# Two weight loads cut into three uneven pieces each, in a kernel of sparse attention and a spectral mix

## The chip, the cores and the metric

The kernel runs on one core of a Trainium2 chip. The metric is the device time of one execution in microseconds (us), as the median of several runs. The kernel before takes 432.17 us (three runs, 431.75 to 432.61). A further execution was profiled; its span, from the first to the last instruction, is 430.2 us. The engines are named as in the profile: PE is TensorE, DVE is VectorE, ACT is ScalarE, POOL is GpSimd and SP is SyncE.

## What is computed

Eight batches of eight heads go through a causal sparse attention. Four heads look at a local band and four at every 32nd position. The result is the input of a spectral mix. A Fourier transform runs along the sequence, 64 complex modes are each multiplied by a 512 by 512 complex matrix of their own, and the transform is inverted. A last product with `w_ch` follows.

```python
def _moe_ref(x, w_r, w_i, w_ch):                 # x: the attention's output, 8 x 576 x 512
    n_modes = w_r.shape[0]                       # 64
    X = np.fft.rfft(x, axis=1)
    Xr, Xi = (np.real(X[:, :n_modes]), np.imag(X[:, :n_modes]))
    Yr = np.einsum('bmd,mde->bme', Xr, w_r) - np.einsum('bmd,mde->bme', Xi, w_i)
    Yi = np.einsum('bmd,mde->bme', Xr, w_i) + np.einsum('bmd,mde->bme', Xi, w_r)
    Y[:, :n_modes] = Yr + 1j * Yi
    y = np.fft.irfft(Y, n=S, axis=1)
    u = x + y
    return u + np.maximum(u @ w_ch, 0.0)
    # ... cut: the attention, the shapes and the scaling of the inputs
```

The matrices `w_r` and `w_i` come as 32-bit numbers, 64 of 512 x 512 each. They are the bulk of what has to be read.

## The kernel before

The weights are loaded on GpSimd's queue, in pairs of modes and in halves of the input rows, and become 16-bit numbers on the way. A pair's tile has the real part on partitions 0 to 63 and the imaginary part on partitions 64 to 127. One load brings one part of one pair to 64 partitions: two modes of 4 rows of 512 numbers, that is 2 x 4 KB on a partition and 512 KB in all.

```python
    SPLIT1, SPLIT0 = 56, 48
    ORDER = [(1, m) for m in range(SPLIT1)] + [(0, m) for m in range(SPLIT0)]
    ORDER += [(1, m) for m in range(SPLIT1, NM)] + [(0, m) for m in range(SPLIT0, NM)]

    def w_fetch(n=1):
        for _ in range(n):
            i = len(w_tiles)                     # goes up by two with each pair
            if i >= 2 * NM:
                return
            half, m = ORDER[i]
            # ... cut: wt, the pair's tile, comes from a pool of five or from a borrowed place
            single = []
            for ri, src in enumerate((moe_w_r, moe_w_i)):
                dst = wt[ds(64 * ri, 64)]
                rows = src[m : m + 2, ds(256 * half, 256), :].rearrange(
                    "m (p c) e -> p m (c e)", c=4
                )
                dst = dst.rearrange("p m c e -> p m (c e)")
                ones = range(2)
                if ri and not m:
                    ones = [1]
                elif i < 2 * NM - 4:
                    nc.gpsimd.dma_start(dst, rows)          # L178
                    continue
                single += [(j, ri, dst[:, j], rows[:, j]) for j in ones]
            for _, _, to, rows in sorted(single, key=lambda x: x[:2]):
                nc.gpsimd.dma_start(to, rows)               # L182: one mode alone
            w_tiles.extend((wt[:, 0], wt[:, 1]))
```

A mode multiplies with sixteen small products and afterwards asks for the next pair:

```python
    def mode(slot, m):
        # ... cut
        for e in range(4):
            for c in range(4):
                nc.tensor.matmul(                           # L557
                    yv[:, mi, e, :],
                    wt[pr, XC[c], ds(128 * e, 128)],
                    Xh[half][pr, c, :, :, m],
                    start=(c == 0), stop=(c == 3),
                )
        if m % 2 and (slot or m // 2 not in GUEST):
            w_fetch()
        # ... cut
```

The inputs of the attention are loaded on the same queue. Those of the strided heads come as 64 partitions and, for every second batch, as 8 partitions more; those of the local heads come as 128 partitions.

```python
            if nb == 2:
                nc.gpsimd.dma_start(two[0:64], src[0:64])            # L210
            else:
                nc.gpsimd.dma_start(ring[0:64, n, :], src[0:64, b % 2])  # L212
            if b % 2 == 0:
                nc.gpsimd.dma_start(two[64:72], src[64:72])          # L214
    # ... cut: the local heads' load (L221), 128 partitions of 1152 numbers
```

Towards the end, modes and the work on the output rows alternate:

```python
    rest = [(0, m) for m in range(SPLIT1, NM)] + [(1, m) for m in range(SPLIT0, NM)]
    for i, (slot, m) in enumerate(rest):
        mode(slot, m)
        # ... cut: the next piece of the work on the output rows
    # ... cut: the last modes' spectra, the last product, the sums and the stores
```

Of the kernel before, what the change touches and what calls it, by code (L numbers as in the profile page):

```python
# [56 lines left out]
def kernel(  # L57
# [10 lines left out]
    nc = tc.nc  # L68
# [79 lines left out]
    SPLIT1, SPLIT0 = 56, 48  # L148
    ORDER = [(1, m) for m in range(SPLIT1)] + [(0, m) for m in range(SPLIT0)]
    ORDER += [(1, m) for m in range(SPLIT1, NM)] + [(0, m) for m in range(SPLIT0, NM)]  # L150
    w_tiles = []
    w_chs = {}
    w_ch = big.tile([128, 4, DM], F16, name="w_ch")

    def w_fetch(n=1):
        for _ in range(n):
            i = len(w_tiles)
# [3 lines that stand above are left out]
            if i // 2 in GUEST:  # L161
                wt = big.tile([128, 2, 4, DM], F16, tag=GUEST[i // 2], name="wt")
            else:
                wt = pw.tile([128, 2, 4, DM], F16, tag="w", name="wt")
# [9 lines that stand above are left out]
                ones = range(2)  # L174
                if ri and not m:
                    ones = [1]
                elif i < 2 * NM - 4:
                    nc.gpsimd.dma_start(dst, rows)  # L178
                    continue
                single += [(j, ri, dst[:, j], rows[:, j]) for j in ones]  # L180
            for _, _, to, rows in sorted(single, key=lambda x: x[:2]):
                nc.gpsimd.dma_start(to, rows)  # L182
            w_tiles.extend((wt[:, 0], wt[:, 1]))
# [362 lines left out]
    def mode(slot, m):  # L546
# [17 lines left out]
        if m % 2 and (slot or m // 2 not in GUEST):  # L564
            w_fetch()
# [144 lines left out]
    strided_tokens()  # L710
    load_str(2, 2)
    w_fetch()

    def str_front(b):
# [35 lines left out]
    for b in range(B):  # L750
        if b in (1, 3):
            load_str(b + 3, 2)
        load_loc(*[(), (), (), (), (0,), (1, 2), (3,), (4, 5)][b])
        w_fetch([2, 1, 1, 1, 1, 1, 0, 0][b])
        front = str_front(b + 1) if b + 1 < B else loc_front(0)
        for t in range(6):
            str_scores(b, t)
            if b > 0:
                if t < 2:
                    str_values(b - 1, 4 + t)  # L760
                elif t == 2:
                    dft(b - 1, 1)
            if t >= 2:
                str_values(b, t - 2)
            for w in front[SPLIT[t] : SPLIT[t + 1]]:
                w()
        if b == 1:
            nc.vector.memset(PL[:, 0:PS0], 0.0)
            fourier(0)
# [8 lines left out]
    for b in range(B):  # L778
# [12 lines left out]
        n = 0  # L791
        nm = NMODES[b]
        for mi in range(nm):
# [3 lines left out]
            n = upto  # L797
# [66 lines left out]
    n = 0  # L864
    for m in range(SPLIT0):
# [4 lines left out]
        n = upto  # L870
# [125 lines left out]
    n = 0  # L996
    NL = len(rest) - 2
    for i, (slot, m) in enumerate(rest):
# [4 lines left out]
        n = upto  # L1003
# [76 lines left out]
```

## Time and profile before

| | |
|---|---|
| time, median of 3 runs | 432.17 us |
| span of the profiled execution | 430.2 us |
| mean granted TensorE clock | 0.894 |
| busy: PE, DVE, ACT, POOL | 344.0, 236.3, 203.5, 107.4 us |
| moved by DMA | 91.78 MB, 213 GB/s in the mean |
| loads of pairs (L178): real, imaginary | 62 and 60 issues of 512 KB |
| issue to landing of those, median | 18.1 and 19.4 us |

The page cuts the span into 40 equal slices, of 10.75 us each. Its DMA row gives the mean busy share of the core's sixteen DMA engines in tenths, and the row below it what they moved. The chain that ended last is followed back from the last instruction, at each step to what released it. A line of the waits names the engine and line that waited, what it waited for, the total, the number of times and the longest one. In the chain told in order of time, a line has the start, the length and the work. The trace further keeps the time of every arrival that a load counts, and the start, length and bytes of every packet on a DMA queue, without the number of the DMA engine.

### The profile page before, as it was taken

Reading aid. Unit: us, or ns where it says so; the run is one execution under the profiler, and the core shown is the slowest. Engines: PE = TensorE matmul, PEld = TensorE weight load, DVE = VectorE, ACT = ScalarE, POOL = GpSimd, SP = SyncE. Lnnn points to the kernel's source line nnn. Section 1 sums busy time; section 2 is a strip of 40 time slices with the busy share of each in tenths; the row PEclk is TensorE's granted clock in tenths of the full one; section 3 lists DMA queues with packets and bytes.
Section 4 is the critical chain, followed back from the end, with each engine's and each line's share of the span. In section 5 each row is a group of like instructions: output and inputs, shape, how many; then the busy total and the mean of one; then the engine's idle time right before and its main releaser. Section 6 shows DMA issues by size and latency. Waiting matters only on the chain.

```text
span 430.2 us, 12274 instructions
## 1 busy us (share of the span) xinstructions
PE 344.0 (80%) x5420; PEld 238.3 (55%) x5420; DVE 236.3 (55%) x461; ACT 203.5 (47%) x357; POOL 107.4 (25%) x191
## 2 busy tenths in 40 slices
PE   2977878779988697898577767786897988888994
PEld 2865767658767575666345545454564544444331
DVE  3888778835544444534104334864684484444695
ACT  1777777634655354547131212522342463432773
POOL 8333332322432222221222221222222222210000
PEclk9999989955998889969755689999899998999998
DMA  8999999999999999999999999999999999992698
GB/s 150 213 213 213 214 214 210 212 210 212 214 213 214 214 213 214 213 214 211 214 214 214 214 213 214 213 214 213 213 213 213 214 214 214 213 206 53 223 353 304
DMA packets 30484, 91.78 MB, mean 213 GB/s; under 512 B 4000, under 2 KB 4768, under 8 KB 30432
## 3 DMA queue, kind: packets, MB, share of 16 engines
q0 software_dynamic: 24704, 81.28, 95.3%
q1 hardware_dynamic: 5216, 9.52, 6.2%
q8 instruction: 42, 0.69, 0.6%
q10 hardware_dynamic: 512, 0.21, 0.2%
q14 instruction: 10, 0.08, 0.0%
HBM read 162.83 MB, written 9.44 MB: 400 GB/s over the span
## 4 chain that ended last, share of the span: by engine, by line
DMA 69%; PE 20%; DVE 5%; issue 2%; ACT 2%; POOL 1%; DVEq 0%; ACTq 0%; POOLq 0%
DMA wt<-in_moe_w_i_dram 52%; DMA ring<-in_q_dram 7%; DMA ring<-in_v_dram 4%; DMA wt<-in_moe_w_r_dram 4%; PE y L557 3%; PE v L935 2%; PE u L945 2%; DMA ring<-in_k_dram 2%; PE v L958 1%; DVE yy L692 1%; PE sc L524 1%; PE sc L657 1%; DVE xb L233 1%; PE tp L405 1%; ACT v L243 1%
## 5 line engine op out<-in xcount | busy, mean ns | idle before, releaser
L557 PE MATMUL y<-X,wt 128*128 128x16 f16 (+1 forms) x2048 | 82.6, 193 | 37.1 <-DMA wt<-in_moe_w_i_dram 35.7
L557 PEld LDWEIGHTS <-wt 128*128 128x128 f16 (+1 forms) x2048 | 72.9, 102 | 51.4 <-issue 41.2
L178 POOL DMA_DIRECT2D wt<-in_moe_w_r_dram x62 | 36.4, 587 | 155.8 <-PE y L557 75.4
L178 POOL DMA_DIRECT2D wt<-in_moe_w_i_dram x60 | 35.4, 589 | 60.3 <-DMA wt<-in_moe_w_i_dram 49.7
L666 ACT ACTIVATE v<-sc 128x512 f16<-128x512 f32 x32 | 19.1, 597 | 64.9 <-PE sc L657 64.9
L481 ACT ACTIVATE PL<-sc 128x480 f16<-128x480 f32 (+1 forms) x48 | 27.2, 579 | 34.0 <-PE sc L467 33.7
L667 DVE COPY xo<-tp 128x512 f16<-128x512 f16 x32 | 22.1, 690 | 32.9 <-PE tp L665 32.8
L657 PE MATMUL sc<-w_cp,xT 128*128 128x512 f16 x128 | 38.3, 425 | 1.3 <-DVE xT L630 1.3
L233 DVE TENSOR_TENSOR xb<-av,rec 90x256 f16<-90x256 f32 (+2 forms) x80 | 36.0, 450 | 2.7
L232 DVE RECIPROCAL rec<-av 90x4 f32<-90x4 f32 (+2 forms) x80 | 14.6, 183 | 34.1 <-PE av L496 24.8
L412 DVE COPY qT<-tp 128x576 f16<-128x576 f16 x16 | 12.1, 758 | 33.4 <-PE tp L405 29.9
L904 DVE TENSOR_TENSOR xo<-u,xo 128x1024 f16<-128x1024 f32 x16 | 19.5, 1224 | 16.3 <-PE u L700 16.3
L243 ACT ACTIVATE v<-tp 128x640 f16<-128x640 f16 (+1 forms) x24 | 19.4, 808 | 19.0 <-PE tp L439 16.3
L405 PE MATMUL tp<-cI_s,ring 64*64 64x64 f16 x864 | 25.0, 204 | 2.0 <-issue 1.2
L370 ACT ACTIVATE PL<-sc 90x360 f16<-90x360 f32 (+1 forms) x48 | 22.8, 490 | 7.5 <-PE sc L363 7.1
L243 ACT ACTIVATE v<-v 128x1024 f16<-128x1024 f32 x16 | 16.4, 1025 | 19.4 <-PE v L700 19.3
L980 DVE TENSOR_TENSOR osb<-u,rl 128x1024 f32<-128x1024 f32 (+1 forms) x21 | 22.2, 1071 | 5.5 <-PE u L958 3.4
L451 PE MATMUL sc<-cMl_s,cI_s 128*128 128x480 f16 (+1 forms) x48 | 20.5, 426 | 3.6 <-ACT PL L481 2.0
L405 PEld LDWEIGHTS <-ring 64*64 64x64 f16 x864 | 19.5, 117 | 6.9 <-issue 2.9
L268 PE MATMUL tp<-cI_s,ring 72*128 72x72 f16 x256 | 15.3, 207 | 9.0 <-DMA ring<-in_v_dram 7.5
L972 ACT ACTIVATE rl<-v 128x1024 f32<-128x1024 f32 (+1 forms) x21 | 18.8, 902 | 6.6 <-PE u L958 4.1
L524 PEld LDWEIGHTS <-xb 108*128 108x128 f16 (+2 forms) x176 | 14.6, 103 | 11.6 <-DVE xb L233 7.1
(134 smaller groups left out, 696.2 us busy)
## 6 DMA issues: line engine op xcount, KB each, us to landing
wt<-in_moe_w_r_dram POOLq DMA_DIRECT2D x62, 512.0 KB, 18.1
wt<-in_moe_w_i_dram POOLq DMA_DIRECT2D x60, 512.0 KB, 19.4
out_dram<-osb SPq DMA_DIRECT2D x15, 512.0 KB, 3.2
ring<-in_v_dram POOLq DMA_DIRECT2D x8, 288.0 KB, 13.2
ring<-in_q_dram POOLq DMA_DIRECT2D x8, 288.0 KB, 13.6
ring<-in_k_dram POOLq DMA_DIRECT2D x8, 288.0 KB, 13.1
ring<-in_v_dram POOLq DMA_DIRECT2D x3, 512.0 KB, 14.8
ring<-in_q_dram POOLq DMA_DIRECT2D x3, 512.0 KB, 14.7
```

Source lines behind the costliest of these rows:

```text
L178: nc.gpsimd.dma_start(dst, rows)
L233: nc.vector.tensor_tensor(out=dst, in0=val.rearrange("p h (q c) -> p h c q", c=4), in1=rec[0:n, 0:pieces] .to_broadcast((n, pieces, 64)) . ...
L243: nc.scalar.activation(out=out, in_=in_, func=ACTF.Copy)
L370: nc.scalar.activation(out=PS[0:n, ds(POFF[t], 4 * n)], in_=scp[0:n, 0 : 4 * n], func=ACTF.Exp, scale=SCALE,)
L405: nc.tensor.transpose(tp[ds(64 * hp, 64), ds(64 * i, 64)], qn[ds(64 * hp, 64), ds(64 * (9 * g + i), 64)], idn[ds(64 * hp, 64), ds(64 * hp, ...
L451: nc.tensor.matmul(scp[:, 0 : n * times].rearrange("p (h x) -> p h x", h=times), idn, mask_rows("cMl", n, times), start=True, stop=False,)
L481: nc.scalar.activation(out=dst, in_=src, func=ACTF.Exp, scale=SCALE)
L557: nc.tensor.matmul(yv[:, mi, e, :], wt[pr, XC[c], ds(128 * e, 128)], Xh[half][pr, c, :, :, m], start=(c == 0), stop=(c == 3),)
L657: nc.tensor.matmul(vp, xT[:, ch], w_chs["cp"][:, ch, :], start=(ch == 0), stop=(ch == 3),)
L667: nc.vector.tensor_copy(out=xo.rearrange("p (h q c) -> p h q c", h=2, c=4), in_=tp[:, 0:512].rearrange("p (h c q) -> p h q c", h=2, c=4),)
L904: nc.vector.tensor_tensor(out=xo, in0=up[:, 0:n], in1=xo, op=AluOp.add)
L980: nc.vector.tensor_tensor(out=osb[:, j], in0=up[:, j], in1=rl[:, j], op=AluOp.add)
```

## The change

The real part of two pairs, the one that is fetched at index 56 and the one at index 86 of the order of modes, is no longer loaded by one transfer of 64 partitions. It is loaded by three, of 35, 20 and 9 partitions and of 7, 49 and 8. The same bytes go to the same places in the same order. The change is for the way in which a transfer is shared out among the DMA engines[...].

```diff
@@ -148,6 +148,7 @@
     ORDER += [(1, m) for m in range(SPLIT1, NM)] + [(0, m) for m in range(SPLIT0, NM)]
+    UNEVEN = {56: (35, 20, 9), 86: (7, 49, 8)}
     w_tiles = []
@@ -174,6 +175,12 @@
                 if ri and not m:
                     ones = [1]
+                elif i in UNEVEN and not ri:
+                    a = 0
+                    for n in UNEVEN[i]:
+                        nc.gpsimd.dma_start(dst[a : a + n], rows[a : a + n])
+                        a += n
+                    continue
                 elif i < 2 * NM - 4:
                     nc.gpsimd.dma_start(dst, rows)
                     continue
```

## The prediction

> **What bounds the kernel now.** I read the chain that ended last first, then the DMA rows, then who waits for whom in the last third, then the landings of single transfers.
>
> The page's chain, by engine and by line, and its DMA rows with the queues:
>
> ```profile
> DMA 69%; PE 20%; DVE 5%; issue 2%; ACT 2%; POOL 1%; DVEq 0%; ACTq 0%; POOLq 0%
> DMA wt<-in_moe_w_i_dram 52%; DMA ring<-in_q_dram 7%; DMA ring<-in_v_dram 4%; DMA wt<-in_moe_w_r_dram 4%; PE y L557 3%; PE v L935 2%; PE u L945 2%; DMA ring<-in_k_dram 2%; PE v L958 1%; DVE yy L692 1%; PE sc L524 1%; PE sc L657 1%; DVE xb L233 1%; PE tp L405 1%; ACT v L243 1%
> ...
> DMA  8999999999999999999999999999999999992698
> GB/s 150 213 213 213 214 214 210 212 210 212 214 213 214 214 213 214 213 214 211 214 214 214 214 213 214 213 214 213 213 213 213 214 214 214 213 206 53 223 353 304
> ...
> q0 software_dynamic: 24704, 81.28, 95.3%
> q8 instruction: 42, 0.69, 0.6%
> ```
>
> The stream of loads through GpSimd's queue (q0) is the bound: 213 GB/s without a hole until slice 36 (about 385 us), 69% of the chain. Nearly all of it is the weight pairs. The small line on q8 matters here: 42 packets of 16 KB (0.69 MB) that fetch instructions on the same sixteen DMA engines.
>
> The chain in order of time near the end of the loads:
>
> ```profile
> 344.12 19.38 DMA wt<-in_moe_w_i_dram
> 363.50 0.28 issue
> 363.79 19.38 DMA wt<-in_moe_w_i_dram
> 383.16 0.14 issue
> 383.30 0.64 PE y L557 x16
> ```
>
> The mode at 383.30 starts 0.14 us after a weight half has landed. From there TensorE works almost without a gap to the end at 430.2. So the landing at 383.16 sets the end, and 47.0 us (430.2 less 383.16) come after it whatever happens. Between 290 and 384 us TensorE does wait:
>
> ```profile
> PE y L557 <- DMA wt<-in_moe_w_i_dram: 11.3, 13, 2.1
> POOL wt L182 <- DMA wt<-in_moe_w_i_dram: 7.0, 4, 1.9
> ```
>
> That is 11.3 us in 13 waits, about 0.87 us each, one for nearly every pair of modes. TensorE follows the landings, so a shift of all landings there is a shift of the end.
>
> **How one transfer lands.** Each load counts sixteen arrivals, one from each DMA engine, and it is landed with the last. The trace keeps these arrivals. For an imaginary part early on they lie between 65.94 and 68.44 us, within 2.5 us. For the imaginary part that landed at 383.16 they begin at 376.26 and the offsets are 0, 0.46, 0.58, 0.71, 1.13, 1.46, 1.66, 2.72 and then 6.04, 6.07, 6.35, 6.41, 6.44, 6.47, 6.59, 6.91. Eight engines are ahead and eight lag by 5 to 7 us, though each got the same bytes. The packet records say why. A 4 KB packet starts every 0.305 us on an engine. At 53.89 us an instruction fetch takes 948 ns exactly where one engine's next packet was due, and that engine is 1.12 us late from then on. About five such fetches fall on each of eight engines: 5 x 1.12 = 5.6 us, the lag seen. So even shares end unevenly, and the last engine sets every landing. The mean of the sixteen offsets is 3.75 us, so perfect shares would gain 6.91 - 3.75 = 3.2 us.
>
> [...] The trace agrees for the 8-partition loads (L214): each puts two packets on eight engines and none on the other eight, and the next takes the other eight. [...] the next transfer's packet starts 21 ns after the packet that counts the arrival.
>
> **The change part by part.** The order of instructions on every engine stays; two loads on GpSimd become six.
>
> *More issues.* Each is 0.587 us by the row of L178, so four more cost GpSimd 2.3 us. GpSimd has only waits there. Eight semaphores go round the loads, so a load waits for the eighth before it; three pieces hold three of them, and for a while the queue holds six full loads instead of eight. Six times the 2.45 us from landing to landing is 14.7 us of stock, more than the 7 us between the first and the last engine. I book zero.
>
> *Moved shares.* [...] Normally an engine gets 4 partitions of such a load. [...] A partition is two packets, 0.61 us. So six engines get 3.05 us more, one 1.22 us, and eight get 2.44 us less.
>
> *If engines 8 to 15 are the laggards*, the largest lag falls to 6.91 - 2.44 = 4.47 us, and the six leaders go to at most 1.46 + 3.05 = 4.51 us. That is balanced to 0.04 us, so it is surely the intention: end 2.4 us earlier, 429.8 us.
>
> *But are they?* I followed the sixteen packet series through the 8-partition loads at 55 to 63 us, when five engines had had a fetch. Two of the five were in the group that L214 takes first (engines 0 to 7), three in the other. The later fetches that I could follow went to the other group, apart from one that I could not settle. So I count two laggards, perhaps three, among engines 0 to 7. Only engines 0 and 7 there are spared the 3.05 us. A laggard at 6.1 to 6.4 us that gets it stands at 9.2 to 9.5 us: 2.3 to 2.6 us over 6.91. Then the landing at 383.16 comes at 385.6 and the end 2.4 us later, 434.6 us.
>
> **The rivals.**
> 1. Laggards hit (weight 0.50): 434.6 us. For it: the group membership above. Against it: the near perfect balance of the other reading, which looks like a design made from a profile[...].
> 2. Laggards relieved (0.35): 429.8 us. For it: the balance. Against it: my count.
> 3. Nearly nothing (0.15): 432.5 us. The two laggards sit at engines 0 and 7 and get 0 and 1.22 us[...].
> 4. Starved leaders: if three pieces at a time emptied the queue, the DMA row would show a hole near 220 or 290 us and the end would be later by its length, up to 2 us. The stock of 14.7 us speaks against it; it is in the upper tail.
>
> **Range and chances.** The weighted sum is 0.50 x 434.6 + 0.35 x 429.8 + 0.15 x 432.5 = 432.6 us. I put the prediction a little nearer to the likeliest outcome, at 433.2 us. The range must hold both directions, with half a microsecond beyond each: 429.4 to 435.6 us. Two per cent are 8.6 us, and the shares moved are worth 3.05 us at most, so within 2% has 0.96 and either side 0.02.
>
> **What would show the steps right or wrong.** The bytes on q0 stay 81.28 MB, with more issues in the table of DMA issues. The groups of TensorE, VectorE and ScalarE keep their counts and mean durations. The chain must still go through the weight loads to a mode about 47 us ahead of the end. If the laggards were hit, the arrivals of the last loads spread over 9 us or more and the landing now at 383.16 is near 385.6. If they were relieved, the spread is below 5 us and it is near 380.8. [...] A hole in the DMA row at the pieces would make the zero for the issues wrong. A shift of the landing that the end does not follow would refute the 47.0 us.

## The result and the profile after

The changed kernel takes 434.45 us, median of 6 runs (433.75 to 434.96), beside 432.17 us for the kernel before (6 runs). The ratio is 1.005 with a 95% interval of 1.0037 to 1.0063, so the change costs 2.28 us (1.6 to 2.7). The time is 1.25 us above the 433.2 us predicted, inside the range, and 0.15 us from the 434.6 us of the first rival.

The page after, first its chain by engine, then the DMA rows, the packets and two queues:

```profile
DMA 31%; PE 12%; DVE 2%; ACT 1%; issue 1%; POOL 0%; DVEq 0%; ACTq 0%; POOLq 0%
...
DMA  8999999999999999999999999999999999991698
GB/s 154 204 212 212 214 215 210 212 210 212 214 212 213 214 215 213 214 214 212 209 213 214 214 213 215 213 212 214 212 214 214 214 214 214 213 195 28 221 355 298
DMA packets 30836, 91.78 MB, mean 212 GB/s; under 512 B 4352, under 2 KB 5120, under 8 KB 30784
q0 software_dynamic: 25056, 81.28, 95.1%
q8 instruction: 42, 0.69, 0.6%
```

The smaller 31% is no gain: the chain is now followed back only to 223 us, where it breaks off. The bytes of q0 are the same, and no slice near 220 or 290 us has a hole. The dip of the slices 35 and 36 is deeper (195 and 28 for 206 and 53 GB/s): the stream ends unevenly, and later. The number of packets under 512 B has grown from 4000 to 4352; the kernel before has

```profile
DMA packets 30484, 91.78 MB, mean 213 GB/s; under 512 B 4000, under 2 KB 4768, under 8 KB 30432
```

The chain of the changed kernel in order of time, near the end of the loads:

```profile
346.61 19.41 DMA wt<-in_moe_w_i_dram
366.30 19.35 DMA wt<-in_moe_w_i_dram
385.65 0.14 issue
385.78 0.64 PE y L564 x16
```

The same transfer as before lands at 385.65 in place of 383.16, and its mode starts 0.13 us after it. From there to the end are 432.8 - 385.65 = 47.15 us. TensorE pays for it in the waits between 290 and 386 us, with 13.3 us in 13 waits where it had 11.3:

```profile
PE y L564 <- DMA wt<-in_moe_w_i_dram: 13.3, 13, 2.9
```

**The sixteen arrivals of that transfer.** They are compared by their distance from their own mean, so that a shift which all sixteen share drops out. In us, sorted, from the arrivals that the traces keep; the second line is a second execution of the unchanged program (below):

```
before       -3.75 -3.29 -3.17 -3.04 -2.62 -2.29 -2.09 -1.03   2.29 2.32 2.60 2.66 2.69 2.72 2.84 3.16
empty table  -3.54 -3.49 -3.42 -2.66 -2.57 -2.45 -1.29 -1.08   1.71 1.95 2.57 2.58 2.60 2.95 2.97 3.19
changed      -5.58 -4.71 -3.42 -2.40 -0.03  0.04  0.13  0.18   0.60 0.74 0.87 0.90 1.39 1.56 4.74 4.98
```

Eight early and eight late arrivals have become two very late ones, ten crowded within 1.6 us in the middle, and four early ones. In the trace of the changed kernel most of this stands at the second of the two loads: from the first arrival of a load to its last it is 6.22 us for the one that lands at 289.30 us and 9.54 us for the one at 296.15, where the kernel before goes from 5.78 us (291.17) to 6.84 (294.69). The shift of 2.49 us of the landing has three parts: 1.82 us more distance of the last arrival from the mean (4.98 less 3.16), 0.29 us by which the mean came later once the pieces had run, and the rest, nearly 0.4 us, of which this execution already stood 0.31 us behind before the first piece was issued.

### The profile page after: what moved, and what is told of

Read it like the earlier page. It is cut to its first block, busy times and chain, and to the rows that moved or that the text cites. A ratio compares the mean times of both kernels' runs of the same rounds, so it can differ in the third digit from the quotient of the medians.

```text
span 432.8 us, 12280 instructions
## 1 busy us (share of the span) xinstructions
PE 345.0 (80%) x5420; PEld 238.5 (55%) x5420; DVE 236.6 (55%) x461; ACT 203.4 (47%) x357; POOL 109.3 (25%) x195
## 2 busy tenths in 40 slices
DMA packets 30836, 91.78 MB, mean 212 GB/s; under 512 B 4352, under 2 KB 5120, under 8 KB 30784
## 5 line engine op out<-in xcount | busy, mean ns | idle before, releaser
L185 POOL DMA_DIRECT2D wt<-in_moe_w_r_dram x60 | 34.9, 582 | 139.7 <-PE y L564 70.5
## 6 DMA issues: line engine op xcount, KB each, us to landing
ring<-in_v_dram POOLq DMA_DIRECT2D x8, 288.0 KB, 13.3
```

## The experiments

Unless a diff says otherwise, each is the changed kernel with another table. `UNEVEN` gives the pieces by index of the load. Ratios are to the kernel before, timed beside it, with the 95% interval.

### Even pieces

```diff
-    UNEVEN = {56: (35, 20, 9), 86: (7, 49, 8)}
+    UNEVEN = {56: (32, 16, 16), 86: (16, 32, 16)}
```

> The same two loads are still three pieces each, but (32, 16, 16) and (16, 32, 16) partitions: every count is a multiple of 16[...]. Theory (shares moved onto two engines that were already late): the end stays at that of the kernel before, 432.2 us within 0.4 us; two arrivals above 9 us do not appear in the last transfers, whose spread stays at 6.9 us; the page counts 64 more packets under 512 B than before (four more completion counts of 16) where the changed kernel has 352 more. Rival (the four extra issues, or six transfers in place of two, cost the time): 434.4 us, as in the changed kernel.

Measured: 433.51 us (14 runs), ratio 1.0028 (1.0018 to 1.0039). The packet line of its page, and its chain:

```profile
DMA packets 30548, 91.78 MB, mean 212 GB/s; under 512 B 4064, under 2 KB 4832, under 8 KB 30496
```

```profile
365.51 19.38 DMA wt<-in_moe_w_i_dram
385.03 0.64 PE y L564 x16
```

The count of 4064 is the 64 more that were expected, and no arrival is more than 3.8 us over the mean. Yet 1.2 us are lost, which neither theory had. The trace shows where: 159 of the 4 KB packets between 202 and 300 us took more than 0.332 us, up to 0.72, where the kernel before has 20 such. 139 of them stand between 285 and 295 us, at the second load. The excess of the 159 over 0.324 us is 14.35 us more than that of the 20, or 0.90 us per engine; the mean of the arrivals comes 0.73 us later across the pieces. So pieces cost time here without a very late arrival; the slower packets are of the size to account for it.

### Single partitions as labels

```diff
+    UNEVEN = {66: 8 * (1,) + (56,), 74: 8 * (1,) + (56,), 82: (1, 1, 1, 1, 55, 5)}
```

> The uneven triples are taken out; in their place twenty pieces of a single partition[...]. Theory (two late engines among positions 1 to 6, six among 8 to 15): positions 0 and 7 are early, exactly two of 1 to 6 are late, and six of 8 to 15 are late; [...]the end is within 1.2 us of 432.2 us. Rival (engines 8 to 15 are all late, the changed kernel lost its time otherwise): all of 0 to 7 early.

Measured, one execution: 443.89 us. It failed as a label, and its loss has another cause than the change's. A single piece stood out in two of the sixteen arrivals. In the first load the pieces that could be followed (five in a row) all moved the same two, as far as the sorted arrivals can be matched: two move by about 0.3 us a piece, the other fourteen by 0.15 to 0.22. So no engine was named. The page has 4720 packets under 512 B. The DMA rows of its page:

```profile
DMA  8999999999999999999995987999999999995598
GB/s 152 206 212 212 214 214 210 214 208 214 212 212 214 214 215 213 213 214 211 214 213 98 196 178 141 214 197 213 213 213 214 213 214 213 213 213 103 205 350 300
```

98, 178 and 141 GB/s in the slices 21, 23 and 24, and between 240 and 241 us not one packet starts. The loads of the traces count on eight semaphores in turn; that eight tiny pieces hold all of them and the queue runs empty is my reading of the hole. This is what the fourth rival looks like, and the changed kernel has nothing of it.

### The empty table

```diff
+    UNEVEN = {}
```

> The changed kernel with an empty table: no load is cut, so its instructions are those of the kernel before. In the first two experiments and in the changed kernel the loads stood 0.3 to 0.4 us later than before already ahead of the first cut load. If that is how executions differ, this kernel's time is 432.2 us within 0.3 us, and its loads may stand anywhere within half a microsecond of those of before. If the profiled execution of before is typical and every cut program starts later, the loads of this one stand within 0.1 us of before.

Measured: 432.11 us (13 runs), ratio 0.9999 (0.9987 to 1.0011). Its loads stand 0.27 us ahead of those of before from the start on, those of the changed kernel 0.31 us behind. That is how executions differ, and it is taken off wherever a mean is compared below.

### Two even halves

```diff
+    UNEVEN = {56: (32, 32), 86: (32, 32)}
```

> Both loads in two even pieces of 32 partitions: two extra issues, all shares even, no piece of 16 partitions. In the first experiment some 140 packets near 285 to 292 us took 0.33 to 0.72 us where 0.32 us is usual. Theory (the slow packets belong to pieces of few partitions[...]; issues and extra completions cost nothing): no slow packets here, and the time of the kernel with the empty table within 0.4 us. Rival (each extra transfer costs about 0.3 us by itself): half of the first experiment's loss, about 432.8 us.

Measured: 432.13 us (13 runs), ratio 0.9995 (0.9986 to 1.0004); 20 slow packets, as before. Its packet line and chain:

```profile
DMA packets 30516, 91.78 MB, mean 213 GB/s; under 512 B 4032, under 2 KB 4800, under 8 KB 30464
```

```profile
363.74 19.38 DMA wt<-in_moe_w_i_dram
383.25 0.64 PE y L564 x16
```

Two more transfers, 32 more completion counts, and the landing where it was. An extra transfer of this size costs nothing here. That does not carry over to tiny ones: the single partitions above moved even the fourteen arrivals that did not stand out by 0.15 to 0.22 us each.

### Larger pieces as labels

```diff
+    UNEVEN = {64: (39, 20, 5), 68: (36, 21, 7), 72: (24, 7, 33), 76: (39, 20, 5), 80: (20, 11, 33)}
```

> A second attempt[...] with larger pieces so that the queue does not run dry: loads 64, 68, 72, 76 and 80 in three pieces of 5 to 39 partitions[...]. [...] Theory (two late engines among positions 1 to 6): two of those six are late, 0 and 7 are early, one of 8 and 9 and five of 10 to 15 are late. [...] Time between 432 and 434.5 us; it is not compared.

Measured, one execution: 434.01 us. The packet times were to name the engines, but 237 packets between 226 and 300 us were slow, by 0.11 us in the mean, and the series could not be told apart. Inconclusive. The page has 512 packets under 512 B more than that of the kernel before, for ten transfers more:

```profile
DMA packets 30996, 91.78 MB, mean 212 GB/s; under 512 B 4512, under 2 KB 5280, under 8 KB 30944
```

### The pattern turned: three kernels

The same six pieces in another order, and another five, ask whether it matters which shares the late engines get, by the number of very late arrivals alone. That needs no series of packets. The positions in the expectations are my estimate of where the shares fall. The traces keep no number of the engine and do not show it.

```diff
+    UNEVEN = {56: (9, 20, 35), 86: (8, 49, 7)}     # reversed
+    UNEVEN = {56: (8, 49, 7), 86: (9, 20, 35)}     # swapped
+    UNEVEN = {56: (15, 49), 86: (9, 35, 20)}       # minus
```

> The same six counts with the pieces of each triple in reverse order: (9, 20, 35) and (8, 49, 7). [...] Theory (shares moved onto engines that were already late): the number of arrivals more than 4.5 us later than the mean of the sixteen, of the transfer that sets the end, is the number of late engines among 3 to 8, and each of these stands 3.05 us later than without pieces. If the two late engines of the lower half are 1 and 2 there is none, the last arrival is at most 2.0 us over the mean in place of 3.2, and the end is 430.3 to 431.5 us; with one or two it is 434.1 to 434.8 us. Rival (six uneven transfers cost their time whatever engines they fall on): 434.4 us and two late arrivals again.

> The reversed triples in exchanged places: (8, 49, 7) for the first load and (9, 20, 35) for the second. [...] Theory: [...]four to six arrivals stand more than 4.5 us over the mean where the changed kernel has two; the last arrival is 6.2 us over the mean, the end 435.0 to 435.8 us. Rival (uneven transfers cost their time whatever engines they fall on): 434.4 us and two late arrivals.

> Pieces of (15, 49) and (9, 35, 20), five transfers[...]. Theory: the number of arrivals more than 4.5 us over the mean is the number of late engines among 15 and 0 to 5. None if the late ones of the lower half are just position 6 and one more that is not below 6, which the changed kernel's two rule out, so at least one: 434.1 to 435.5 us. Together with the reversed pieces this says which positions of 1 to 6 are late. Rival (uneven transfers cost their time whatever engines they fall on): 434 us and two late arrivals.

Measured: reversed 435.16 us, ratio 1.0066 (1.0054 to 1.0078); swapped 436.53 us, 1.0096 (1.0082 to 1.0111); minus 434.43 us, 1.0055 (1.0042 to 1.0068). The arrivals, as above:

```
reversed     -5.80 -5.35 -3.96 -1.45 -0.98 -0.30 -0.18  0.03   0.23  0.74 0.96 1.08 1.86 2.48 5.32 5.32
swapped      -4.57 -4.39 -4.31 -4.22 -3.86 -3.65 -3.51 -2.62  -0.68 -0.57 5.03 5.14 5.14 5.15 5.92 5.98
minus        -4.71 -4.36 -0.32 -0.27 -0.22 -0.04  0.05  0.11   0.20  0.34 0.65 0.67 0.72 0.76 1.55 4.86
```

Two, six and one very late arrivals, each within what the theory gave: none to two, four to six, at least one. The rival, for which it is all the same where the pieces fall, expected two each time; it is refuted by the count alone. (In the swapped kernel the last of the sixteen lands at 387.34 us.) Which engines these are is not shown; the map of the next two expectations puts the counts and my estimate of the positions together. The landings follow, here of the reversed kernel and of the one called minus, for 383.16 before:

```profile
366.13 19.34 DMA wt<-in_moe_w_i_dram
385.61 0.64 PE y L564 x16
```

```profile
366.10 19.33 DMA wt<-in_moe_w_i_dram
385.57 0.64 PE y L564 x16
```

The swapped kernel, and less the reversed one, are 0.7 and 0.4 us above what was expected. For the swapped one 156 slow packets are a reason: the mean of its arrivals comes 1.17 us later across the pieces. For the reversed one, with 35 of them and 0.15 us, it stays open.

### The pattern fitted to the map

```diff
+    UNEVEN = {56: (15, 25, 24), 86: (15, 25, 24)}  # early
+    UNEVEN = {56: (25, 24, 15), 86: (25, 15, 24)}  # early4
```

> The map that the last three experiments give: 9 to 14 late (six late arrivals when they had the five), 6 and one of 3, 4 and 5 late (two late arrivals with 3 to 8, one with 15 and 0 to 5), the others early. Both loads in pieces of (15, 25, 24)[...]. Theory: if 3 is not the late one, no arrival is more than 3 us over the mean; the late engines come 1.22 us earlier against it, the last arrival is about 2.0 us over the mean in place of 3.2, and the end is 1.2 us earlier less what slow packets cost (0.1 to 0.9 us as measured in the other triples): 431.0 to 431.9 us, below the kernel before. If 3 is the late one, one arrival at 5.1 us over the mean and 434 us. Rival (uneven transfers cost their time whatever engines they fall on): 434.4 us.

> The same aim with other pieces: (25, 24, 15) and (25, 15, 24)[...]. Theory: if 5 is the late one of 3, 4 and 5 (so that the late ones are 5, 6 and 9 to 14), no late arrival, the last 2.0 us over the mean and the end 431.0 to 431.9 us; if 4 is the late one, one arrival 5.7 us over the mean and 434.5 us. Rival (uneven transfers cost their time whatever engines they fall on): 434.4 us.

Measured: 431.45 us (13 runs), ratio 0.9989 (0.9981 to 0.9997), and 431.41 us (21 runs), ratio 0.9985 (0.9978 to 0.9992). The arrivals, and the chain of the first:

```
early        -4.88 -4.49 -4.16 -0.34 -0.19  0.27  0.35  0.72   0.93 0.96 1.39 1.69 1.79 1.80 1.87 2.30
early4       -4.36 -4.30 -3.91 -0.29 -0.20  0.02  0.51  0.57   0.76 1.18 1.31 1.33 1.42 1.62 2.10 2.25
```

```profile
363.07 19.38 DMA wt<-in_moe_w_i_dram
382.59 0.64 PE y L564 x16
```

No very late arrival in either: the last is 2.30 and 2.25 us over the mean. That is what the map let expect, with 5 as the late one of 3, 4 and 5; the map itself stays an estimate. Both kernels beat the one before, by 0.5 and 0.65 us on the ratio, and the changed one by 3 us, with pieces of the same kind. The last arrival came 0.86 and 0.91 us nearer to the mean, and 0.36 us of it went back because the pieces made the mean later.

### Neighbouring partitions against a comb

```diff
+    UNEVEN = {56: (16, 16, 16, 16), 86: (16, 16, 16, 16)}   # four
```

```diff
+    UNEVEN = (56, 86)                                       # comb
-                    a = 0
-                    for n in UNEVEN[i]:
-                        nc.gpsimd.dma_start(dst[a : a + n], rows[a : a + n])
-                        a += n
+                    for a in range(4):
+                        nc.gpsimd.dma_start(dst[a:64:4], rows[a:64:4])
```

> Both loads in four even pieces of 16 neighbouring partitions[...], eight transfers in place of two. It is half of a pair that asks where the slow packets of the earlier experiments come from. Theory[...]: many slow packets near the two loads, over 100 more than the 20 that the kernel before has between 202 and 300 us, and an end 0.5 to 2 us later than 432.1 us. Rival (the source rows of these two loads, or the time at which they run): about as many slow packets here as in the other half of the pair.

> The same eight transfers of 16 partitions, but each takes every fourth partition (0, 4, 8 ... 60, then 1, 5, 9 ... and so on)[...]. Theory[...]: the slow packets are gone, 20 give or take 10 between 202 and 300 us, and the time is 432.1 us within 0.4 us. Rival (each extra transfer costs time): the same loss as with neighbouring partitions.

Measured: four 433.17 us (12 runs), ratio 1.0023 (1.0012 to 1.0034), with 149 slow packets between 202 and 300 us; comb 432.41 us (12 runs), ratio 1.0007 (0.9998 to 1.0016), with 34, a few more than the 10 to 30 expected. Their rows of GB/s, first four, then comb:

```profile
GB/s 155 209 212 213 213 213 212 212 211 212 214 213 213 214 214 214 213 214 212 212 213 214 214 214 214 213 205 212 213 213 214 214 213 213 214 205 48 219 353 305
```

```profile
GB/s 151 211 212 213 214 212 213 210 211 212 214 211 213 215 213 214 214 214 212 211 211 213 214 214 215 213 212 214 214 213 214 213 214 213 214 209 53 221 355 303
```

The dip to 205 GB/s in slice 26 (280 to 291 us) is gone with the comb. The same eight transfers of the same size lose most of their cost when the partitions are spread (by the ratios 1.0 us over the kernel before against 0.3), so the number of transfers is not most of what costs. The source rows are spread along with the partitions, and which of the two it is was not shown. And in both kernels with neighbouring partitions nearly all slow packets belong to the load at 86 and hardly any to the one at 56, though both are cut alike; why stays open.

## Why the prediction was right

**The bound and the 47 us: right.** The landing was to come at 385.6 if laggards were hit; it came at 385.65, and the end followed by 47.15 us. That it fits to 0.05 us is partly luck, since 0.31 us of the landing's shift was there before the first piece. TensorE's waits grew by 2.0 us.

**The shares: an estimate, borne out by the arrivals.** The traces keep no number of the engine. For the 8-partition loads the sixteen series of packets in the kernel before, followed one by one, tell who takes part: pairs of 4-byte packets stand in eight of them between 55.1 and 56.9 us, in the other eight between 58.2 and 60.1, and in the first eight again from 60.7 to 62.5, each 5.56 us later. For the uneven pieces this was not followed, so which engines they run on is not shown. The shares of the prediction, 3.05 us more for six engines and 2.44 us less for eight, are my estimate; only the time of a partition under them, two packets of 0.305 us, is measured. They are tested by the very late arrivals: two, and two, six, one, none and none in the five kernels with other uneven pieces, each within what was expected. The small packets tell even pieces from uneven ones. Two even halves bring 32 packets under 512 B for two more transfers and the even triples 64 for four, sixteen for each. The changed kernel has 352 more for four, so 288 beyond that. Its trace has the surplus at the two loads: 124 packets of 4 bytes and about 9 ns between 210 and 218 us and 163 between 282 and 294 us, where the kernel before has none between 200 and 300. The pieces of the kernel called early bring 320 more for four transfers, 256 beyond the sixteens:

```profile
DMA packets 30804, 91.78 MB, mean 214 GB/s; under 512 B 4320, under 2 KB 5088, under 8 KB 30752
```

**Laggards hit: right in the number.** Two laggards, perhaps three, were counted among engines 0 to 7 from the packets of 55 to 63 us, and two arrivals are very late, at 4.74 and 4.98 us over the mean. Which engines they belong to is not shown. That an instruction fetch makes an engine late, which the prediction read from one case (948 ns, then 1.12 us late), is seen more often in the traces. In the kernel before, the distance from the first arrival of a transfer to its last grows in steps of about 1.1 us, from 2.5 us at 83 us over 3.6, 4.8 and 5.8 to 6.9 us at 303 us; the steps follow the fetches that start at 88.12, 142.56, 198.36 and 292.36 us and take 0.97 to 0.98 us. In the kernel with single partitions, whose arrivals had come together, one arrival jumps out after the fetch at 304.5 us, to 1.8 us over the mean, and a second after the one at 315.2 us, to 1.6. No kernel without the fetches was run.

**The size: right in its sum, of two terms that were each off.** The step said that a laggard at 6.1 to 6.4 us gets 3.05 us and stands 2.3 to 2.6 us over the old last one. Measured against the mean, the last arrival went out by only 1.82 us. The 3.05 us fits if the two that were hit are the two least late of the eight. Those stand at 1.71 and 1.95 with the empty table and at 2.29 and 2.32 in the kernel before; plus 3.05 that is 4.76 to 5.37, and the changed kernel has 4.74 and 4.98, the reversed one, with two very late arrivals as well, 5.32 twice. So what was mis-sized is where the two stood: by this match 0.8 to 1.5 us under the last, where the prediction took 0.5 to 0.8. The match is argued, and executions differ by half a microsecond in it. Part of what is missing came from the term that was booked at zero.

**"I book zero" for the pieces: right for issues, wrong for the transfers.** Two halves cost nothing (ratio 0.9995), and nothing starved. But the pieces made the mean of the arrivals 0.29 us later: 69 slow packets with 2.9 us more excess than before, 0.18 us per engine; what makes up the rest is not shown. So 1.82 + 0.29 = 2.1 us, where 2.28 (1.6 to 2.7) were measured. That two terms, one too large and one too small, add up so well is luck.

**The weights: this cost the 1.25 us.** The arrival counts already spoke for the first rival, and the fine balance of the second (4.47 against 4.51 us) was read as its author's intention. A balance says what somebody may have meant, not which engine is late. The balance also took all of 0 to 7 for early, which my own count of packets denied. And it was not as fine as it looked: the 4.51 us holds only if the two least early of the eight, at 1.66 and 2.72 us, are the engines 0 and 7, which nothing showed; with the one at 2.72 among the six it is 5.77 us. With the first rival alone the prediction would have been 434.6 us.

## What to carry to other kernels

In this kernel a load lands with the last of sixteen arrivals, 6.91 us after the first. Uneven pieces cost or gained by their sizes and their order: the six timed tables with them run from 431.41 to 436.53 us, 3 us between the changed kernel and the better fitted one, of which that one gains only 0.5 us of 432. Here the pattern was turned and the arrivals that come out late were counted (two, six and one) before it was fitted. Pieces that still spread over the partitions lost little (432.41 us for the comb, 433.17 for the neighbours), and single partitions cost most (443.89 us, with 98 GB/s in one slice).

## What the runs showed of the hardware that was not expected

- Pieces of 16 neighbouring partitions have packets of up to 0.72 us for 0.32. The pair of kernels with and without neighbours has 149 slow packets against 34. That hardly any of the 149 belong to the first of the two loads is not explained by it.
- The uneven pieces of the changed kernel bring 288 packets under 512 B beyond the sixteen of each transfer, of 4 bytes; most often they follow each other at 6 ns.
- Single-partition pieces moved the same two arrivals five times running, by about 0.3 us a piece where the others move by 0.15 to 0.22. Why is open.
- In the kernel with single pieces, whose queue ran dry (98 GB/s in a slice), the sixteen arrivals, 5.2 us apart ahead of them, were within 0.71 us after the second load of them. The one execution was 11.8 us longer.
